# Retention scores by 8 products of 64x128 instead of 16 on quarters of the array, with the keys in their order

## The chip, the cores and the metric

The kernel runs on one core of a Trainium2 chip. The metric is device time in microseconds (us) for one execution of the whole program. One execution was also profiled: its trace tells for each engine when each instruction began and ended and what it waited for.

## What is computed

Retention attention for 8 batches, 8 heads, 576 tokens and 64 numbers a head, then a layer of 8 experts on the result, in float32:

```python
scores = scale * np.matmul(q, k.transpose(0, 1, 3, 2))
gamma = 1.0 - 2.0 ** (-5.0 - np.arange(H, dtype=np.float32))
rel = pos[:, None] - pos[None, :]
Dmat = np.where(rel >= 0, gamma[:, None, None] ** rel[None, :, :], 0.0)
ret = scores * Dmat[None, :, :, :]
x = np.matmul(ret, v)                       # then tokens x 512
# experts: rows with x @ w_skip > 0 go to the expert e with the largest x @ w_gate,
# and get x + gate * (relu(x @ w1[e]) @ w2[e]); the others stay x
```

## The kernel before

The 8 x 576 = 4608 tokens are 36 tiles of 128 tokens (NT). Nine tiles (NPD) hold one pair of sequences, so the middle tile of a pair (place 4) holds the end of one sequence and the start of the next. Each tile g is one step of a loop that is unrolled in the program; the order of the TensorE instructions is the order in which the program is written. After the 36 steps, at about 150 us, come the experts, which take the rest of the time and which the change leaves alone.

A step g issues to TensorE, in this order: `state(g)` (L668, keys by values, summed into the state of the sequence; it does nothing at the last tile of a pair), `values(g)` (L688, masked scores by values), `carried(g)` (L709, the state of earlier tiles by queries; it does nothing at the first tile of a pair), `scores(g + 2)` (L618, keys by queries), `stage_c(g - 1)` (L739, four transposes of the finished tile to rows), `flush` (L234, L237, L322, L332: routing matmuls that VectorE has prepared), `logits_b` (L762, four transposes, in every fourth step) and `logits_a` (L747, in every fourth step). VectorE multiplies the scores by the causal mask on their way from the accumulators psc to SBUF (`causal`) and the results by the decay (`decayed`), and does the routing in the time between. GpSimd scales the values (`scale`, L653). ScalarE copies the state, the transposed rows (L741, and sends them to HBM) and the logits lt (L756).

The scores of a step are 8 heads with 64 numbers each. Two heads share the 128 partitions (r = 0, 1, the upper and the lower 64 rows of the array), and for each of four such pairs (a) the 128 keys are taken in two halves of 64 (c), so that 16 products of 64 keys by 128 or 64 queries use the four 64x64 quarters of the array; a half of the keys that lies behind the first 64 queries is left out (k0). For odd a the keys' halves are swapped: `rows` swaps the tokens of k and v on the host, `_tables` swaps the decay of the values, and the mask has a second plane for it. A float32 product is two MATMUL instructions, each with a load of weights, in the trace.

Loads: `load` sends one DMA of 512 KB for q and k by head (n = 0, six buffers) and one for v and k by token (n = 1, four buffers), on SP's queue in the order of the program: v of tile g + 4 after `values(g)`, q of tile g + 6 after `carried(g)`. The keys by token are read by `state` alone.

Of the kernel before, what the change touches and what calls it, by code (L numbers as in the profile page):

```python
# [11 lines left out]
F32 = mybir.dt.float32  # L12
# [5 lines left out]
ALU = mybir.AluOpType  # L18
# [3 lines left out]
B, H, S, D = 8, 8, 576, 64  # L22
NTOK, DM, NE, DF = B * S, H * D, 8, 1024
P = 128
NT = NTOK // P
NQ = S // D
NPR = H // 2
NPD = 2 * S // P
# [41 lines left out]
def kernel(  # L70
# [9 lines left out]
    nc = tc.nc  # L80
# [15 lines left out]
    def keep_up(n):  # L96
        for _ in range(n):
            nc.tensor.matmul(ps_m, warm[:, :P], warm, start=True, stop=True)
# [26 lines left out]
        out=utri, in_=utri, compare_op=ALU.is_gt, fill=0.0, base=0, pattern=[[1, P]], channel_multiplier=-1  # L125
# [56 lines left out]
    def vec(name, *args, **kw):  # L182
        ins = getattr(nc.vector, name)(*args, **kw)  # L183
        if pinned[0]:
            tc.keep_in_program_order(ins)
        return ins
# [6 lines left out]
    def flush(most=None):  # L193

        n = len(adds) if most is None else most
        for do in pe + adds[:n]:
            do()
        pe.clear()
        del adds[:n]
        flushed[0] += 1  # L200
# [342 lines left out]
    with ExitStack() as actx:  # L543
        ac = actx.enter_context(tc.tile_pool(name="ac", bufs=1))
# [9 lines left out]

        q_t, v_t = {}, {}

        def load(into, n, g):
            into[g] = ap.tile([P, 2, DM], F32, tag="qv"[n], name=f"{'qv'[n]}_{g}", bufs=(QBUFS, VBUFS)[n])
            nc.sync.dma_start(into[g].rearrange("p s i -> p (s i)"), qkv[g, n])

        load(q_t, 0, 0)
        nc.scalar.dma_start(tt_sb, ttab)
        load(v_t, 1, 0)
# [9 lines left out]
        masks = []  # L573

        def make_mask(n):
            m = ac.tile([P, 2, P], F32, tag=f"mask{n}", name=f"mask{n}")
            tc.keep_in_program_order(nc.gpsimd.memset(m, 1.0))
            for e in range(2):
                for c in range(2):
                    part = m[c * D : (c + 1) * D, e, :]  # L580
                    if n and c == e:
                        tc.keep_in_program_order(nc.gpsimd.memset(m[c * D : (c + 1) * D, e, D:], 0.0))
                        part = m[c * D : (c + 1) * D, e, :D]
                    ins = nc.gpsimd.affine_select(
                        out=part,
                        in_=part,
                        compare_op=ALU.is_ge,
                        fill=0.0,
                        base=-D if c != e else 0,
                        pattern=[[1, part.shape[-1]]],  # L590
                        channel_multiplier=-1,
                    )
                    tc.keep_in_program_order(ins)
            masks.append(m)

        make_mask(0)
# [2 lines left out]
        halves = [slice(0, D), slice(D, P)]  # L599
        sc_t, st_t, xt_t = {}, {}, {}  # L600
        psc = [pp.tile([P, NPR, P], F32, tag=f"sc{r}", name=f"psc{r}") for r in range(2)]
        for r in range(2):
            nc.vector.memset(psc[r], 0.0)

        def head(a, r):
            return 2 * a + (r ^ (a & 1))

        def place(g):
            return g % NPD

        def scores(g):

            q = q_t[g].rearrange("p s (a i) -> p s a i", a=NPR)
            for a in range(NPR):
                for c in range(2):
                    k0 = D * (c ^ (a & 1))
                    for r in range(2):
                        nc.tensor.matmul(  # L618
                            psc[r][halves[c], a, k0:],
                            q[halves[r], 1, a, k0 : k0 + D],  # L620
                            q[halves[r], 0, a, k0:],
                            start=a == 0,
                            stop=a == NPR - 1,
                            skip_group_check=True,
                        )

        def causal(g):

            sc_t[g] = ap.tile([P, 2, NPR, P], F32, tag="sc", name=f"sc_{g}", bufs=AHEAD_SC + 1)
            m = masks[place(g) == NPD // 2].unsqueeze(1).broadcast_to([P, NPR // 2, 2, P])  # L630
            for r in range(2):
                vec(
                    "tensor_tensor",
                    sc_t[g][:, r].rearrange("p (b e) i -> p b e i", e=2),
                    psc[r].rearrange("p (b e) i -> p b e i", e=2),
                    m,
                    ALU.mult,
                )
# [21 lines left out]
        def state(g):  # L660

            t = place(g)
            if t == NPD - 1:
                return
            v, k = (v_t[g][:, s].rearrange("p (h i) -> p h i", h=H) for s in range(2))
            for a in range(NPR):
                for r in range(2):
                    nc.tensor.matmul(  # L668
                        ps_s[halves[r], a, :],
                        k[:, head(a, r), :],  # L670
                        v[:, head(a, r), :],
                        start=t in (0, NPD // 2) and a == 0,
                        stop=a == NPR - 1,
                        skip_group_check=True,
                    )
            st_t[g + 1] = ap.tile([P, NPR, D], F32, tag="st", name=f"st_{g + 1}")
            nc.scalar.copy(st_t[g + 1], ps_s)
# [149 lines left out]
        def lower_whole(f):  # L827
            hi, lo = wq[0, f]
            vec("tensor_tensor", lo, chunks[f], hi.bitcast(F32), ALU.subtract)
# [14 lines left out]
        def closed(b, pn):  # L844

            logits_c(b, pn)
            if (b + 1) * NB in starts:
                k = starts.index((b + 1) * NB) - 1
                post = (lambda: close_first(ps_m, starts[KCUT + 1] * P)) if k == KCUT else None
                work.append(route(ps_m, k, post))  # L850
# [18 lines left out]
        for g in range(NT):  # L869
            last = g >= NT - 2  # L870
            if g < len(NKEEP):
                keep_up(NKEEP[g])
            state(g)
            pxt = values(g)
            if g == NT - 3:
                lower_whole(3)
            if g + VBUFS < NT:
                load(v_t, 1, g + VBUFS)
            carried(g, pxt)
            if g + QBUFS < NT:  # L880
                load(q_t, 0, g + QBUFS)
            old = len(adds) if g < (KCUT + 4) * NB else None
            if last:
                decayed(g, pxt)
            if pn is not None:
                closed(g // NB - 1, pn)
                pn = None
            if g < NT - 1:
                spare(SPARE if g < (KCUT + 4) * NB else LATE)
            if not last:  # L890
                first = decayed(g, pxt)
                scale(g + 2, first)
                lower(1, first)
            if g == NT - 3:
                lower_whole(4)
            score(g + (AHEAD_SC if g > 2 else 1))
            if g < 4:
                decays(g + 1)
            if g:
                stage_c(g - 1)  # L900
            if g != NT - 2:
                flush(old)
            if lt is not None:
                pn = logits_b(g // NB - 1, lt)
                lt = None
            if g and g % NB == 0:
                lt = logits_a(g // NB - 1)
            weights()
        g = NT
# [509 lines left out]
def _tables():  # L1419
    gam = 1.0 - 2.0 ** (-5.0 - np.arange(H, dtype=np.float64))  # L1420
    a = np.arange(NPR)
    gtab = np.zeros((P, 2, NPR, D))
    qtab = np.zeros((P, NQ + 1, NPR))
    off = D * (np.arange(NQ + 1) % NQ - np.arange(NQ + 1) % 2)
    for j in range(2):
        mine = slice(j * D, (j + 1) * D)
        g = gam[2 * a + j]
        for c in range(2):
            gtab[mine, c] = g[None, :, None] ** (c * D + np.arange(D))[None, None, :] / np.sqrt(D)
        qtab[mine] = g[None, None, :] ** off[None, :, None]  # L1430
    pos = np.arange(NPD * P).reshape(NPD, P) % S
    vtab = gam[None, None, :] ** -pos.T[:, :, None]
    odd = np.arange(H) // 2 % 2 == 1
    vtab[:, :, odd] = np.roll(vtab, D, axis=0)[:, :, odd]
    f = np.float32
    ttab = np.concatenate([vtab.reshape(P, -1), qtab.reshape(P, -1)], axis=1)
    return gtab.reshape(P, DM).astype(f), ttab.astype(f)
# [41 lines left out]
```

## Time and profile before

| | us |
|---|---|
| median of 3 runs | 395.24 |
| lowest and highest | 391.83, 397.61 |
| the profiled execution | 394.96 |
| its span, first to last instruction | 393.3 |

The span is shorter than the execution by 1.7 us that lie around it. In the rows further below, times are us from the span's start unless marked ns. PE is TensorE's matmuls, PEld its loads of weights, DVE VectorE, ACT ScalarE, POOL GpSimd, SP SyncE; a name with q is the engine's sequencer or DMA queue. L618 is line 618 of the kernel before. "x16" is a count of instructions. Matmuls overlap, so a group's time from its own start to the start of the next group is a better measure of what it costs than its busy time.

### The profile page before, as it was taken

How to read it: one execution, taken by the hardware profiler on the slowest of the kernel's cores; microseconds unless marked ns; L12 is line 12 of the kernel's file. 1: busy time of each engine (PE TensorE's matmuls, PEld its weight loads, DVE VectorE, ACT ScalarE, POOL GpSimd, SP SyncE). 2: the span in 40 equal slices, each digit the busy share in tenths (PEclk: the TensorE clock that was granted, in tenths of full speed). 3: DMA queues.
4: the chain of work that ended last, by engine and by line, in shares of the span. 5: the costliest groups of instructions: out<-in, count | busy, mean ns of one | idle time of the engine just before them, and what ended most of it. 6: DMA issues, size and time to landing. Idle time of an engine off the chain costs nothing.

```text
span 393.3 us, 11952 instructions
## 1 busy us (share of the span) xinstructions
PE 376.0 (96%) x4792; PEld 342.1 (87%) x4792; DVE 280.4 (71%) x690; ACT 149.6 (38%) x258; POOL 162.0 (41%) x183
## 2 busy tenths in 40 slices
PE   8889999999899999999999999999999999999992
PEld 4768788787787877888999999999999999999992
DVE  3765695596379998967753887597787887977625
ACT  1222322232234435128432545445445455464210
POOL 5532232223144463160123347328448348660712
PEclk9999999999899999999999999999999999999998
DMA  8999999999999936175899997687877878973101
GB/s 301 405 413 351 354 343 310 391 353 319 412 323 350 358 112 215 67 243 153 259 317 258 300 245 201 241 231 243 250 236 255 219 247 271 254 236 122 48 9 58
DMA packets 41001, 101.00 MB, mean 257 GB/s; under 512 B 5165, under 2 KB 14129, under 8 KB 40944
## 3 DMA queue, kind: packets, MB, share of 16 engines
q1 hardware_dynamic: 31440, 80.62, 62.5%
q0 software_dynamic: 4032, 10.03, 7.7%
q10 hardware_dynamic: 5472, 9.56, 6.5%
q8 instruction: 39, 0.64, 0.7%
q14 instruction: 18, 0.15, 0.1%
HBM read 81.49 MB, written 19.21 MB: 256 GB/s over the span
## 4 chain that ended last, share of the span: by engine, by line
PE 88%; DVE 5%; DMA 3%; issue 2%; ACT 1%; SPq 0%; POOL 0%; DVEq 0%
PE py L507 28%; PE ph L507 25%; PE pxt L688 8%; PE psc L618 6%; PE ps_s L668 5%; PE px L739 5%; PE pxt L709 4%; PE pl L747 2%; DMA v<-qkv 2%; DMA w<-w 1%; PE ps_m L322 1%; DVE sc L183 1%; PE ph L532 1%; PE pn L762 1%; DVE xt L183 1%
## 5 line engine op out<-in xcount | busy, mean ns | idle before, releaser
L1139 POOL DMA_INDIRECT out<-yq,siq x60 | 72.8, 1213 | 51.0 <-DVE yq L1118 26.7
L170 ACT CAST whi_w<-w 128x1024 fp32r<-128x1024 f32 x59 | 61.8, 1050 | 36.9 <-PE py L507 35.2
L653 POOL TENSOR_TENSOR v<-v,tt_sb 128x512 f32<-128x512 f32 x36 | 37.6, 1043 | 91.4 <-DVE xt L183 67.9
L171 DVE TENSOR_TENSOR wlo_w<-w,whi_w 128x1024 fp32r<-128x1024 f32 x59 | 71.2, 1210 | 2.1 <-ACT whi_w L170 2.1
L507 PE MATMUL py<-hlo,whi_w 128*128 128x344 f32 (+8 forms) x232 | 69.9, 301 | 0.4 <-DVE hlo L520 0.4
L507 PE MATMUL py<-hhi,whi_w 128*128 128x344 f32 (+8 forms) x232 | 69.8, 301 | 0.0
L507 PE MATMUL py<-hhi,wlo_w 128*128 128x344 f32 (+8 forms) x232 | 69.6, 300 | 0.0
L507 PE MATMUL ph<-xhi,whi_w 128*128 128x344 f32 (+6 forms) x224 | 67.8, 303 | 0.0
L507 PE MATMUL ph<-xhi,wlo_w 128*128 128x344 f32 (+6 forms) x224 | 67.7, 302 | 0.0
L507 PE MATMUL ph<-xlo,whi_w 128*128 128x344 f32 (+6 forms) x224 | 67.6, 302 | 0.0
L520 DVE SCALAR_TENSOR_TENSOR hlo<-ph,hhi 128x344 fp32r<-128x344 f32 (+8 forms) x60 | 28.5, 474 | 43.6 <-ACT hhi L519 43.5
L183 DVE TENSOR_TENSOR sc<-psc,mask 128x512 f32<-128x512 f32 x72 | 46.3, 684 | 10.5 <-PE psc L618 6.4
L741 ACT COPY xn<-px 128x512 f32<-128x512 f32 x36 | 21.1, 586 | 82.0 <-PE px L739 73.7
L183 DVE TENSOR_TENSOR xt<-pxt,gt_sb 128x256 f32<-128x256 f32 x72 | 27.0, 417 | 31.8 <-PE pxt L709 29.1
L519 ACT ACTIVATE hhi<-ph 128x344 fp32r<-128x344 f32 (+8 forms) x60 | 25.6, 426 | 57.9 <-PE ph L507 57.9
L420 POOL DMA_INDIRECT xg<-out,gidx x21 | 26.3, 1253 | 47.6 <-issue 27.4
L507 PEld LDWEIGHTS py<-hlo,whi_w 128*128 128x128 f32 x232 | 43.7, 188 | 0.7 <-DVE hlo L520 0.7
L507 PEld LDWEIGHTS py<-hhi,wlo_w 128*128 128x128 f32 x232 | 43.8, 189 | 0.0
L507 PEld LDWEIGHTS py<-hhi,whi_w 128*128 128x128 f32 x232 | 43.7, 188 | 0.0
L507 PEld LDWEIGHTS ph<-xhi,whi_w 128*128 128x128 f32 x224 | 42.2, 188 | 0.1
L507 PEld LDWEIGHTS ph<-xlo,whi_w 128*128 128x128 f32 x224 | 42.1, 188 | 0.1
L507 PEld LDWEIGHTS ph<-xhi,wlo_w 128*128 128x128 f32 x224 | 42.2, 188 | 0.0
(203 smaller groups left out, 601.7 us busy)
## 6 DMA issues: line engine op xcount, KB each, us to landing
w<-w SPq DMA_DIRECT2D x64, 512.0 KB, 4.3
q<-qkv SPq DMA_DIRECT2D x36, 512.0 KB, 7.5
v<-qkv SPq DMA_DIRECT2D x36, 512.0 KB, 6.7
out<-xn ACTq DMA_DIRECT2D x36, 256.0 KB, 5.5
xr<-xg SPq DMA_DIRECT2D x7, 512.0 KB, 5.3
xq<-xr SPq DMA_DIRECT2D x12, 144.0 KB, 4.6
xq<-xr SPq DMA_DIRECT2D x8, 176.0 KB, 5.4
xq<-xr SPq DMA_DIRECT2D x8, 160.0 KB, 6.9
```

The source lines that it names most:

```text
L170: nc.scalar.copy(hi, t)
L171: ins = nc.vector.tensor_tensor(lo, t, hi.bitcast(F32), ALU.subtract)
L183: ins = getattr(nc.vector, name)(*args, **kw)
L420: return nc.gpsimd.indirect_dma_start(out=dst, out_offset=None, in_=out[:nrow], in_offset=bass.IndirectOffsetOnAxis(ap=idx, axis=0), bound ...
L507: nc.tensor.matmul(ps, x, y, start=first and n == 0, stop=ends, skip_group_check=skip)
L519: nc.scalar.activation(hi, ph, AF.Relu)
L520: keep(nc.vector.scalar_tensor_tensor(lo, ph, 0.0, hi.bitcast(F32), ALU.max, ALU.subtract))
L618: nc.tensor.matmul(psc[r][halves[c], a, k0:], q[halves[r], 1, a, k0 : k0 + D], q[halves[r], 0, a, k0:], start=a == 0, stop=a == NPR - 1, s ...
L653: ins = nc.gpsimd.tensor_tensor(v, v, vt_sb[:, place(g), :].unsqueeze(2).broadcast_to([P, H, D]), ALU.mult)
L688: nc.tensor.matmul(pxt[a % 2][halves[j], a // 2, :], v[:, head(a, r), :], sc[:, r, a, :], start=a < 2, stop=t == 0 and a >= NPR - 2, skip_ ...
L741: nc.scalar.copy(xn, px)
L1139: ins = nc.gpsimd.indirect_dma_start(out=dst, out_offset=bass.IndirectOffsetOnAxis(ap=idx, axis=0), in_=rows, in_offset=None, bounds_check ...
```

## The change

The scores become 8 products of 128 keys by 128 queries: for each a and r one product on a 64x128 half of the array, with no part left out. The mask becomes one plane of 128x128, built with one selection. The swap of the keys' halves for odd a goes, on the host (rows of k and v, the decay table) and in the mask; the memsets that cleared the accumulators psc go too. `logits_b` is issued ahead of `flush` instead of behind it. The last tile of each pair (place 8, four of the 36 tiles) loads only v, half of the former transfer.

```diff
         def load(into, n, g):
             into[g] = ap.tile([P, 2, DM], F32, tag="qv"[n], name=f"{'qv'[n]}_{g}", bufs=(QBUFS, VBUFS)[n])
-            nc.sync.dma_start(into[g].rearrange("p s i -> p (s i)"), qkv[g, n])
+            m = 1 if n and place(g) == NPD - 1 else 2
+            nc.sync.dma_start(into[g][:, :m, :].rearrange("p s i -> p (s i)"), qkv[g, n, :, : m * DM])
...
-            m = ac.tile([P, 2, P], F32, tag=f"mask{n}", name=f"mask{n}")
+            m = ac.tile([P, P], F32, tag=f"mask{n}", name=f"mask{n}")
             tc.keep_in_program_order(nc.gpsimd.memset(m, 1.0))
...
+            ins = nc.gpsimd.affine_select(
+                out=m, in_=m, compare_op=ALU.is_ge, fill=0.0, base=0, pattern=[[1, P]], channel_multiplier=-1
+            )
+            tc.keep_in_program_order(ins)
+            if n:
+                tc.keep_in_program_order(nc.gpsimd.memset(m[:D, D:], 0.0))
...
-        for r in range(2):
-            nc.vector.memset(psc[r], 0.0)
...
             for a in range(NPR):
-                for c in range(2):
-                    k0 = D * (c ^ (a & 1))
-                    for r in range(2):
-                        nc.tensor.matmul(
-                            psc[r][halves[c], a, k0:],
-                            q[halves[r], 1, a, k0 : k0 + D],
-                            q[halves[r], 0, a, k0:],
...
+                for r in range(2):
+                    nc.tensor.matmul(
+                        psc[r][:, a, :],
+                        q[halves[r], 1, a, :],
+                        q[halves[r], 0, a, :],
...
-            m = masks[place(g) == NPD // 2].unsqueeze(1).broadcast_to([P, NPR // 2, 2, P])
+            m = masks[place(g) == NPD // 2].unsqueeze(1).broadcast_to([P, NPR, P])
...
-            if g != NT - 2:
-                flush(old)
             if lt is not None:
                 pn = logits_b(g // NB - 1, lt)
                 lt = None
+            if g != NT - 2:
+                flush(old)
...
-    odd = np.arange(H) // 2 % 2 == 1
-    vtab[:, :, odd] = np.roll(vtab, D, axis=0)[:, :, odd]
...
-        odd = np.arange(H) // 2 % 2 == 1
-        return np.where(odd[:, None], np.roll(x, D, axis=1), x).reshape(NT, P, DM)
+        return x.reshape(NT, P, DM)
```

## Rows read from the trace of the kernel before

**Rows 1.** The page: its span, and busy us (share of span) with instructions.

```profile
span 393.3 us, 11952 instructions
PE 376.0 (96%) x4792; PEld 342.1 (87%) x4792; DVE 280.4 (71%) x690; ACT 149.6 (38%) x258; POOL 162.0 (41%) x183
```

**Rows 2.** The page: the chain of work that ended last, by engine.

```profile
PE 88%; DVE 5%; DMA 3%; issue 2%; ACT 1%; SPq 0%; POOL 0%; DVEq 0%
```

**Rows 3.** Stretches: length, each engine's busy time (instructions), granted clock, DMA share, GB/s.

```profile
20.00:146.00 126.00, 120.26 (x2753) 99.64 (x2754) 90.33 (x253) 38.69 (x76) 40.71 (x42) 0.99 0.92 338
...
100.00:120.00 20.00, 18.22 (x396) 15.54 (x397) 11.38 (x34) 6.28 (x12) 6.24 (x7) 0.91 0.98 369
```

**Rows 4.** Waits of TensorE, 20 to 146 us: total, times, longest.

```profile
PE psc L618 <- issue: 4.6, 5, 1.8
PE psc L618 <- DVE sc L183: 1.0, 2, 0.8
```

**Rows 5.** Timeline of TensorE in a clean step: start, length, group.

```profile
53.05 0.67 PE L709 MATMUL pxt<-q,st 64*64 64x128 f32 x16
53.53 0.85 PE L618 MATMUL psc<-q 64*64 64x128 f32 x32
54.31 0.66 PE L739 MATMUL px<-ident,xt 128*128 128x128 f32 x4
54.90 0.39 PE L668 MATMUL ps_s<-v 128*64 128x64 f32 x6
```

**Rows 6.** Timeline of TensorE in a step without L709.

```profile
45.17 1.05 PE L688 MATMUL pxt<-sc,v 128*64 128x128 f32 x16
46.14 0.90 PE L618 MATMUL psc<-q 64*64 64x128 f32 x32
46.98 0.33 PE L739 MATMUL px<-ident,xt 128*128 128x128 f32 x1
```

**Rows 7.** Timeline of TensorE in the last steps, some without scores.

```profile
143.74 0.66 PE L739 MATMUL px<-ident,xt 128*128 128x128 f32 x4
144.23 0.60 PE L762 MATMUL pn<-ident,lt 128*128 128x128 f32 x4
...
146.25 0.67 PE L709 MATMUL pxt<-q,st 64*64 64x128 f32 x16
146.85 0.66 PE L739 MATMUL px<-ident,xt 128*128 128x128 f32 x4
```

**Rows 8.** Timeline around the longest idle stretch of TensorE (in brackets).

```profile
100.42 0.85 PE L618 MATMUL psc<-q 64*64 64x128 f32 x31
...
103.05 0.27 PE L618 MATMUL psc<-q 64*64 64x128 f32 x1 [1.78 <-issue]
...
103.25 1.11 PE L739 MATMUL px<-ident,xt 128*128 128x128 f32 x4
```

**Rows 9.** The page: the instruction queue's packets, MB, share of 16 engines.

```profile
q8 instruction: 39, 0.64, 0.7%
```

**Rows 10.** Instructions of L618 from 20 to 146 us: duration, first and last.

```profile
L618 PE MATMUL psc<-q x1024: 212/267/320, 20.4 to 143.6; 64*64 64x64 f32 x98, 64*64 64x128 f32 x73
```

**Rows 11.** Timeline of the start, GpSimd and VectorE.

```profile
3.59 1.29 POOL L584 TENSOR_SCALAR_AFFINE_SELECT mask<-mask 64x128 f32<-64x128 f32 x4
...
6.41 1.04 POOL L653 TENSOR_TENSOR v<-v,tt_sb 128x512 f32<-128x512 f32 x1 [1.52 <-DMA v<-qkv]
6.46 1.29 DVE L183 TENSOR_TENSOR sc<-psc,mask 128x512 f32<-128x512 f32 x2 [4.11 <-issue]
```

**Rows 12.** Timeline: ScalarE's copy of the logits, and their transposes.

```profile
90.52 0.59 ACT L756 COPY lt<-pl 128x512 f32<-128x512 f32 x1 [0.44 <-PE pl L747]
...
93.63 0.60 PE L762 MATMUL pn<-ident,lt 128*128 128x128 f32 x4
```

More of the change, by code (lines that the diff above doesn't have):

```diff
@@ L555, with place @@
         q_t, v_t = {}, {}
+        def place(g):
+            return g % NPD
         def load(into, n, g):
             into[g] = ap.tile([P, 2, DM], F32, tag="qv"[n], name=f"{'qv'[n]}_{g}", bufs=(QBUFS, VBUFS)[n])
-            nc.sync.dma_start(into[g].rearrange("p s i -> p (s i)"), qkv[g, n])
+            m = 1 if n and place(g) == NPD - 1 else 2
+            nc.sync.dma_start(into[g][:, :m, :].rearrange("p s i -> p (s i)"), qkv[g, n, :, : m * DM])
         load(q_t, 0, 0)
@@ L575, in make_mask @@
         def make_mask(n):
-            m = ac.tile([P, 2, P], F32, tag=f"mask{n}", name=f"mask{n}")
+            m = ac.tile([P, P], F32, tag=f"mask{n}", name=f"mask{n}")
             tc.keep_in_program_order(nc.gpsimd.memset(m, 1.0))
-            for e in range(2):
-                for c in range(2):
[L580 to L593, printed above, removed]
+            ins = nc.gpsimd.affine_select(
[4 more added lines that the diff above has]
+                tc.keep_in_program_order(nc.gpsimd.memset(m[:D, D:], 0.0))
             masks.append(m)
@@ L601 @@
         psc = [pp.tile([P, NPR, P], F32, tag=f"sc{r}", name=f"psc{r}") for r in range(2)]
-        for r in range(2):
-            nc.vector.memset(psc[r], 0.0)
         def head(a, r):
             return 2 * a + (r ^ (a & 1))
-        def place(g):
-            return g % NPD
         def scores(g):
@@ L614, in scores @@
             for a in range(NPR):
-                for c in range(2):
-                    k0 = D * (c ^ (a & 1))
-                    for r in range(2):
-                        nc.tensor.matmul(
-                            psc[r][halves[c], a, k0:],
-                            q[halves[r], 1, a, k0 : k0 + D],
-                            q[halves[r], 0, a, k0:],
[L622 to L625, printed above, removed]
+                for r in range(2):
[3 more added lines that the diff above has]
+                        q[halves[r], 0, a, :],
+                        start=a == 0,
+                        stop=a == NPR - 1,
+                        skip_group_check=True,
+                    )
         def causal(g):
             sc_t[g] = ap.tile([P, 2, NPR, P], F32, tag="sc", name=f"sc_{g}", bufs=AHEAD_SC + 1)
-            m = masks[place(g) == NPD // 2].unsqueeze(1).broadcast_to([P, NPR // 2, 2, P])
+            m = masks[place(g) == NPD // 2].unsqueeze(1).broadcast_to([P, NPR, P])
             for r in range(2):
@@ L633, in causal @@
                     "tensor_tensor",
-                    sc_t[g][:, r].rearrange("p (b e) i -> p b e i", e=2),
-                    psc[r].rearrange("p (b e) i -> p b e i", e=2),
+                    sc_t[g][:, r],
+                    psc[r],
                     m,
```

## The prediction

> **What bounds the kernel now.** First the page's busy times and its chain: TensorE is busy for 376.0 of 393.3 us, and 88% of the chain that ended last is TensorE [rows 1, 2]. So the question is what the change does to TensorE's own queue, and, since it edits only the retention stage, in the tile steps of the first 150 us. The table by stretches shows the steps between 20 and 146 us: TensorE busy 120.26 of 126 us, granted clock 0.99, DMA share 0.92 [rows 3]. Both are near full, so it has to be settled which is waited for. TensorE's list of waits for the same stretch answers: 4.6 us before products of L618 that nothing in the profile released ("issue"), 1.0 us for VectorE's masking, and no line for a load [rows 4]. Loads are late at times, but never late enough for TensorE. The steps are paced by TensorE's instruction stream, and I price the change there.
>
> Now one clean step, read from the starts of TensorE's groups: L709 at 53.05, L618 at 53.53, L739 at 54.31, L668 at 54.90 [rows 5]. The score products hold the queue for 54.31 - 53.53 = 0.78 us, the carried-state products (L709) ahead of them for 0.48. A step without L709 shows L688 from 45.17 to 46.14 = 0.97 us, then L618 from 46.14 to 46.98 = 0.84 [rows 6].
>
> **The shape of the score products.** Before, a step's scores are 32 matmuls (16 calls, two each in float32) on four 64x64 quarters of the array, 64 or 128 queries each. A quarter gets 4 x 2 passes, half of 128 columns and half of 64: 8 x 96 = 768 columns. After, 16 matmuls on two 64x128 halves, all of 128 queries: 8 x 128 = 1024 columns per half. The trace of before has no 64x128 product. The nearest row is L688: also 16 matmuls of 128 columns on two tiles, 0.97 us [rows 6]. From below, no row allows less than the present 0.78, since the columns per tile grow by a third; from above, halves that don't run together would take twice L688, 1.94. I take 0.97: the four quarters of L618 run together today, among them both row halves (32 matmuls in 0.78), which two halves also need. That is 0.97 - 0.78 = +0.19 us a step.
>
> **The change of shape in front.** Today L709 and L618 both use 64x64 tiles. After, L709's 64x64 is followed by 64x128. Where the next group has another shape, a group's tail shows in the rows: L709 ahead of L739 takes 146.85 - 146.25 = 0.60 instead of 0.48, and L739 ahead of L762 (same shape) takes 0.49 against 0.59 ahead of L668, where only the columns of the tile differ [rows 5, 7]. And the group behind a change starts slower: L618 behind L688 takes 0.84, behind L709 0.78 [rows 5, 6]. So a new change of shape costs 0.12 + 0.06 = 0.18 us; from below it costs 0, if tiles of equal rows can follow each other freely, which no row shows. I take 0.18, because L739 to L668 is also a change of columns alone. The Trainium skill has the rule (TensorEngine Tiling (Array Packing), Key Properties): a change of tiling mode, unlike a change of tile within one mode, drains the array. By that rule the 64x64 to 64x128 step drains, which is the value that the rows led to; taken without it the sum would be 5.4 us lower.
>
> **How often.** 36 sets of score products are issued. The first two lie in front of TensorE's wait for the first two loads and cost nothing; if they were on the path, +0.4. Of the 34 others, 30 stand behind L709 (+0.37 each = 11.1), three behind L688, at the tiles that start a sequence pair (+0.19 = 0.6), one behind another set (+0.2): **+11.9 us**. Without the drain 34 x 0.19 = +6.5.
>
> **The gaps.** The 4.6 us of "issue" are five idle stretches, all inside or just ahead of L618, the longest 1.78 [rows 4, 8]. They cost more than their idle time, since the work around them no longer overlaps: the set at 100.42 ends at 103.25, 2.83 - 0.78 = 2.05 for 1.78 idle [rows 8]. I take that surplus, 0.27, for each of the five, an estimate: 4.6 + 1.3 = 5.9. Right behind the longest gap the clock drops: in 100 to 120 us the granted clock is 0.91 [rows 3], so 0.09 x 20 = 1.8 us of full clock are lost, of which I count 1.7. What are the gaps? Nothing releases them, and they fall in the densest part of the instruction stream: 64 instructions (32 loads of weights, 32 matmuls) in 0.78 us. The page lists an instruction queue with 39 packets, 0.64 MB [rows 9], and TensorE has 2 x 4792 = 9584 matmuls and weight loads [rows 1]: if that queue is TensorE's own, 246 in a packet of 16 KB. I read the gaps as late instruction packets, held up in the DMA queues that are 92% busy. Between 20 and 146 us TensorE issues 2753 + 2754 instructions [rows 3], 246 in 5.6 us; after, 1024 fewer (half of the 1024 matmuls of L618 and as many loads [rows 10]) in about 132 us, 246 in 7.2. Each packet has some 1.6 us more to arrive, nearly the longest gap. I take the gaps as gone: **-5.9 - 1.7 = -7.6 us**. From below nothing is regained: 0.
>
> **Costed at nothing.** (a) Four of the 36 v loads bring half: 1 MB less on SP's queue, the order of issue unchanged. It is hidden because TensorE waits for no load [rows 4]; if loads set the pace it would be worth 1.05 MB at 338 GB/s, 3.1 us. (b) The memsets of psc on VectorE and most of the mask on GpSimd (1.29 us) go. GpSimd's first scaling waits 1.52 us for a load behind the mask, and VectorE is idle for 4.11 us ahead of its first masking [rows 11]; without that cover the gain would be about the 1.29 us once. (c) Masking has the same 128x512 elements and the mask is only broadcast differently: 0.65 us as before (1.29 for two [rows 11]); were it slower, VectorE is idle for 126 - 90.33 = 35.7 us between 20 and 146 us, or 1 us a step [rows 3]. (d) logits_b moves ahead of the routing matmuls of flush, on TensorE alone; it issues no DMA. It needs ScalarE's copy lt, which starts at 90.52 and takes 0.59, long before the transposes at 93.63 [rows 12]. Behind it now wait the routing matmuls, 0.5 us later in 8 of 36 steps; their accumulator is read a step or more later. Should lt be late, the whole queue would stand behind it. (e) A longer step gives VectorE, GpSimd and the loads time; it takes none.
>
> **Sum**, against the profiled execution's own 394.96 us (span 393.3; the median of the runs is 395.24, 0.3 more): 394.96 + 11.9 - 7.6 = 399.3 us, +1.1%. Without the drain and with the gaps gone 394.96 + 6.5 - 7.6 = 393.9; with the drain and no gap regained 406.9.
>
> **Rivals.** *The gaps stay* (slower). If the gaps are not owed to the density of L618's instructions, only the costs remain: 394.96 + 11.9 = 406.9, +3%. It decides from about 4 us of gaps kept. For it: the profile names no releaser, and DMA stays above 90% busy. Against: all five lie at L618. The Trainium skill (Runtime: NRT & Kernel Launch, Instruction fetch mechanics) says that instruction fetch is mostly hidden, so that by it the gaps would have another cause and could stay; the rows above place them at the densest stretch, which speaks rather for fetch. *The halves run one after the other* (much slower): 0.97 more a set, 34 x 0.97 = 33, 432 us; against it stands the overlap of the quarters now. *The loads set the pace* (faster): then TensorE's extra time is hidden, 3.1 us of loading and the gaps go: 394.96 - 3.1 - 7.6 = 384.3. Against: no TensorE wait for a load [rows 4]. *No change of shape is felt, or the changes cancel*: 394, inside the forecast's side.
>
> **Chances.** Forecast, costs and regained gaps between 392 and 402.9: 0.55. Gaps stay, wholly or mostly: 0.27. Halves in turn: 0.06. Loads or something else that gives over 2%: 0.12. The likeliest case's own range is 393 to 404; for 8 in 10 I go to 388 below and 408 above, which leaves out the halves in turn and most of the faster case. About 2% (7.9 us) is what a measurement of this kernel can tell from no change: faster 0.11, within 0.56, slower 0.33 (gaps stay, halves in turn).
>
> **What would show it.** L618 with 16 matmuls of 64x128, start to next start near 1.03 us (0.97 + 0.06); L709 ahead of it 0.60; "issue" before L618 under 1 us in all, and no half clock after 20 us; the instruction queue with about 4 or 5 packets fewer (1152 of TensorE's instructions). Wrong would be: L618 at 0.8 or 1.9; gaps of the same sum, at L618 or elsewhere; a new TensorE wait for v or q.

## The result and the profile after

The changed kernel takes 399.39 us (median of 20 runs, 398.55 to 400.24), the kernel before beside it 396.2 (20 runs, 391.83 to 399.89): ratio 1.0095, interval 1.0074 to 1.0116. It is about 1% slower, within the 2% that counted as no change. The profiled execution takes 398.64 us, 3.7 more than that of before. The experiments further below ran on other chips, where the kernel before itself scattered between 394.1 and 412 us; so they are read by their traces first, and by a ratio only where one is given with its interval.

The page after: span, busy time, the instruction queue, the chain that ended last.

```profile
span 396.9 us, 10793 instructions
PE 385.0 (97%) x4216; PEld 347.9 (88%) x4216; DVE 280.0 (71%) x688; ACT 150.0 (38%) x258; POOL 162.6 (41%) x176
...
q8 instruction: 34, 0.56, 0.6%
...
PE 91%; DMA 3%; DVE 2%; issue 1%; ACT 1%; POOL 1%; SPq 0%; DVEq 0%
```

TensorE lost 576 matmuls and 576 loads of weights, the instruction queue 5 packets [rows 1, 9]. VectorE's share of the chain fell from 5% to 2% [rows 2]. Now the tile steps, by stretches as in [rows 3], and TensorE's waits from 20 to 146 us as in [rows 4]:

```profile
20.00:146.00 126.00, 125.04 (x2178) 101.63 (x2178) 88.31 (x245) 37.12 (x74) 38.60 (x40) 1.00 0.91 328
100.00:120.00 20.00, 20.00 (x364) 16.61 (x360) 12.18 (x33) 5.91 (x12) 6.27 (x7) 1.00 1.02 400
```

```profile
PE psc L605 <- DVE sc L183: 0.8, 1, 0.8
```

The 4.6 us of idle time that nothing released are gone, all of them, and with them the drop of the clock: 1.00 in 100 to 120 us, where it was 0.91. TensorE is busy for 125.04 of 126 us instead of 120.26. And still the program is longer, because each step is. A clean step after (L696 is the former L709, L605 the former L618, L726 the former L739, L655 the former L668):

```profile
55.66 0.67 PE L696 MATMUL pxt<-q,st 64*64 64x128 f32 x16
56.26 1.16 PE L605 MATMUL psc<-q 64*128 64x128 f32 x16
57.35 0.66 PE L726 MATMUL px<-ident,xt 128*128 128x128 f32 x4
57.94 0.45 PE L655 MATMUL ps_s<-v 128*64 128x64 f32 x8
```

From start to next start, the carried products take 0.60 us (0.48 before) and the score set 57.35 - 56.26 = 1.09 (0.78 before) [rows 5]. Behind the values' products, where there are no carried ones, the set takes 1.10 (0.84 before, [rows 6]):

```profile
48.07 1.16 PE L605 MATMUL psc<-q 64*128 64x128 f32 x16
49.17 0.65 PE L726 MATMUL px<-ident,xt 128*128 128x128 f32 x4
```

What a set's single instructions last (shortest, median, longest, ns), first before, then after:

```profile
L618 PEld LDWEIGHTS psc<-q x1024: 129/133/136, 20.3 to 143.5; 64*64 64x64 f32 x171
```

```profile
L605 PEld LDWEIGHTS psc<-q x512: 182/188/188, 21.7 to 147.9; 64*128 64x128 f32 x171
L605 PE MATMUL psc<-q x512: 272/272/373, 21.7 to 148.0; 64*128 64x128 f32 x171
```

A load of 128 columns lasts some 53 ns longer than one of 64. In the middle of a set this is hidden behind matmuls; at its start, behind a change of shape, it is not, and the longest matmuls, the first of a set, last 373 ns where they lasted 320 [rows 10].

Where the difference ends: the first product of the experts starts at 154.01 us before and at 158.33 after, 4.3 us later. The profiled executions differ by 3.7, so 0.6 are made up in the experts; where in them was not looked for.

```profile
154.01 0.50 PE L507 MATMUL ph_early<-x,whi_w 128*128 128x256 f32 x2 [0.39 <-DVE x L183]
```

```profile
158.33 0.48 PE L507 MATMUL ph_early<-x,whi_w 128*128 128x256 f32 x2
```

### The profile page after: what moved, and what is told of

It reads as the page before. It is cut to its first block, busy times and chain, and to the rows that moved or that the text cites. A ratio compares the mean times of both kernels' runs of the same rounds, so it can differ in the third digit from the quotient of the medians.

```text
span 396.9 us, 10793 instructions
## 1 busy us (share of the span) xinstructions
PE 385.0 (97%) x4216; PEld 347.9 (88%) x4216; DVE 280.0 (71%) x688; ACT 150.0 (38%) x258; POOL 162.6 (41%) x176
## 4 chain that ended last, share of the span: by engine, by line
PE 91%; DMA 3%; DVE 2%; issue 1%; ACT 1%; POOL 1%; SPq 0%; DVEq 0%
PE py L507 28%; PE ph L507 25%; PE psc L605 9%; PE pxt L675 7%; PE px L726 5%; PE ps_s L655 5%; PE pxt L696 4%; PE pl L734 2%; DMA v<-qkv 2%; DMA xg<-out,gi 1%; PE ph_early L507 1%; PE pn L749 1%; PE ph L532 1%; PE ps_m L322 1%; DVE sc L183 0%
## 5 line engine op out<-in xcount | busy, mean ns | idle before, releaser
L1126 POOL DMA_INDIRECT out<-yq,siq x60 | 74.7, 1245 | 56.2 <-DVE yq L1105 28.9
L605 PE MATMUL psc<-q 64*128 64x128 f32 x576 | 42.3, 285 | 1.0 <-DVE sc L183 0.8
```

The lines of the kernel that those rows point to most:

```text
L605: nc.tensor.matmul(psc[r][:, a, :], q[halves[r], 1, a, :], q[halves[r], 0, a, :], start=a == 0, stop=a == NPR - 1, skip_group_check=True,)
L1126: ins = nc.gpsimd.indirect_dma_start(out=dst, out_offset=bass.IndirectOffsetOnAxis(ap=idx, axis=0), in_=rows, in_offset=None, bounds_check ...
```

## The experiments

Three things had to be told apart: whether the products alone carry the change; whether the shape or the columns make them dearer; and what the idle gaps were. Theory on the gaps: TensorE uses up its instructions faster than packets of them arrive. Rivals: they belong to the products on quarters, or the loads alone make them.

**The rest of the change alone.** The kernel before, with the half loads and `logits_b` ahead of `flush`; scores, masks and layout as before.

```diff
+            m = 1 if n and g % NPD == NPD - 1 else 2
+            nc.sync.dma_start(into[g][:, :m, :].rearrange("p s i -> p (s i)"), qkv[g, n, :, : m * DM])
...
             if lt is not None:
                 pn = logits_b(g // NB - 1, lt)
                 lt = None
+            if g != NT - 2:
+                flush(old)
```

> The kernel before with two parts of the change alone: the half loads of the last tile of a pair and the logits' transposes ahead of the flush; the score products stay on quarters. Theory (the score products carry the whole change): no difference that can be measured, ratio 1.000, TensorE's idle gaps of the kernel before still there (2 to 8 us). Rival (the other parts give something that hides part of the products' cost): 3 us faster (0.992), the price of 1 MB of loads.

Its waits from 20 to 146 us:

```profile
PE psc L619 <- issue: 3.0, 3, 2.1
PE psc L619 <- DVE sc L183: 1.0, 2, 0.8
PE pxt L710 <- issue: 0.4, 1, 0.4
```

The gaps are still there, 3.4 us. The profiled execution took 397.9 us, the kernel before in the same session 396.4 at its lowest. Too few runs could be compared for an interval, so a gain of 3 us is not excluded by the times. The trace shows none: TensorE waits for no load here either. The first product of the experts does start 2.5 us earlier than in the kernel before, but 1.2 us less of gaps and a clock that does not drop (it cost 1.7 us in the kernel before) cover that:

```profile
151.47 0.51 PE L507 MATMUL ph_early<-x,whi_w 128*128 128x256 f32 x2 [0.40 <-DVE x L183]
```

**The same columns on quarters.** The changed kernel with each score product cut in two by its keys: 64x64 again, so no change of shape behind the carried products, but 1024 columns per tile.

```diff
             for a in range(NPR):
-                for r in range(2):
+                for c in range(2):
+                    for r in range(2):
...
-                        psc[r][:, a, :],
-                        q[halves[r], 1, a, :],
-                        q[halves[r], 0, a, :],
+                            psc[r][halves[c], a, :],
+                            q[halves[r], 1, a, halves[c]],
+                            q[halves[r], 0, a, :],
```

> The changed kernel with each score product cut in two by its keys: 16 products of 64 keys by 128 queries on quarters, so again 64x64 like the carried-state products ahead of them, 32 matmuls, but the 1024 columns per tile of the change. Theory (of the 0.43 us a step that the products cost, 0.19 are columns and 0.24 the change of shape and its exposed first load): the carried products 0.48 instead of 0.60, the score set 0.97 instead of 1.09, 30 x 0.24 = 7 us less, 392 us, if the idle gaps stay away; with as many instructions as before some may come back, up to 8 us, then 392 to 400. Rival (the change of shape costs nothing, the columns and the larger weights cost all): score set 1.09, carried 0.60, 399 us.

> 16 products of 64 keys by 128 queries on quarters, all else as in the changed kernel, again, because the first time the runs were disturbed. Theory (change of shape 0.22 us a step, read from the first profile; its instruction rate is nearly that of the kernel before, so gaps of 2 to 4 us): 30 x 0.22 = 6.6 less than the changed kernel, 2 to 4 given back: 3 to 5 us under the changed kernel, ratio to the kernel before about 0.995 to 1.005. Rival (shape costs nothing over the whole program, the next step absorbs it): as the changed kernel, 1.01.

A clean step, from the second profile:

```profile
50.96 0.67 PE L697 MATMUL pxt<-q,st 64*64 64x128 f32 x16
51.45 1.05 PE L606 MATMUL psc<-q 64*64 64x128 f32 x32
52.44 0.65 PE L727 MATMUL px<-ident,xt 128*128 128x128 f32 x4
```

The carried products take 0.49, the set 0.99, together 1.48. With the change it is 1.69, before 1.26. So of the 0.43 us that a step got longer, 0.22 are the third more columns (1.48 - 1.26) and 0.21 the change of shape with its exposed first load (1.69 - 1.48). The load's own part shows behind the values' products, where the shape changes either way (128x64 to 64x64 here, to 64x128 with the change):

```profile
47.41 1.10 PE L606 MATMUL psc<-q 64*64 64x128 f32 x32
48.45 0.66 PE L727 MATMUL px<-ident,xt 128*128 128x128 f32 x4
```

With first loads of 64 columns the set takes 1.04 us there, with 128 columns 1.10: 0.06 for the larger load. The gaps came back in part, in the second profile 1.7 us:

```profile
PE px L727 <- issue: 1.5, 1, 1.5
PE psc L606 <- DVE sc L183: 1.0, 2, 0.8
PE pxt L676 <- issue: 0.2, 1, 0.2
```

In the first session the ratio to the kernel before was 1.0032 (0.9928 to 1.0136, from two runs of this kernel), in the second 1.0068 (1.0019 to 1.0117), just above the upper end of what was expected. The changed kernel itself, beside it in the second session:

> The changed kernel once more, beside the next two, on their chip. Theory: TensorE waits on nothing that the profile does not release before the scores (under 0.5 us of issue between 20 and 146 us), score set 1.09, carried products 0.60, and a ratio to the kernel before of 1.005 to 1.015. Rival (the absence of gaps in the first profile was luck): 2 us of gaps or more.

It came to 1.012 (1.0053 to 1.0188), without a gap in 20 to 146 us, as in its first profile. By medians the quarters with all columns take 2.9 us less (399.36 against 402.24), where 6.6 - 1.7 = 4.9 would be left; the two intervals overlap, so the times alone do not show a difference. What the shape costs is read from the steps.

**More instructions, same shape.** The changed kernel with each product of scores by values cut in two by queries: as many instructions per step as before.

```diff
-                    nc.tensor.matmul(
-                        pxt[a % 2][halves[j], a // 2, :],
-                        v[:, head(a, r), :],
-                        sc[:, r, a, :],
-                        start=a < 2,
+                    for h in range(2):
+                        nc.tensor.matmul(
+                            pxt[a % 2][halves[j], a // 2, halves[h]],
+                            v[:, head(a, r), :],
+                            sc[:, r, a, halves[h]],
+                            start=a < 2 and h == 0,
```

> The changed kernel with each product of scores by values cut in two by queries: 32 matmuls of 64 queries and 32 loads of weights instead of 16 and 16, same columns, same shape, so the instruction count per step is that of the kernel before while the score products stay 64x128. Theory (the gaps are late instruction packets, owed to the density): idle gaps that nothing releases come back, each behind an instruction packet, 1 to 5 us in all, at the dense stretch wherever that now is; 400 to 404 us and a wider spread from run to run. Rival (the gaps belonged to the quarter products themselves or to chance): none, spread as narrow as with the change (under 2 us), 399 to 400 us, if the group of values stays at 0.98 us.

```profile
20.00:146.00 126.00, 125.04 (x2498) 106.09 (x2497) 82.11 (x225) 34.17 (x69) 34.90 (x36) 1.00 0.89 320
```

This missed: no gap came back, and the time rose to between 411.9 and 425.3 us (four runs; the kernel before beside it 396.4 to 412.0). The cut was not free, as had been assumed: the group of values takes 1.24 us instead of 0.98:

```profile
57.73 1.31 PE L676 MATMUL pxt<-sc,v 128*64 128x64 f32 x32
58.97 0.67 PE L697 MATMUL pxt<-q,st 64*64 64x128 f32 x16
```

So the step got longer with its instructions, and the pace fell: 4995 instructions in 126 us, 246 in 6.2 us, against 5.4 before outside its gaps. The count per step alone does not make the gaps. That left two readings, the pace or the quarters, and the next pair tells them apart.

**Products on quarters at a slower pace.** The kernel of the first experiment, where each tile's transposes to rows are issued two or three times with the same result.

```diff
-            for c in range(NCC):
+            for c in 2 * list(range(NCC)):
                 nc.tensor.transpose(px[:, c * P : (c + 1) * P], xt_t[b][:, c, o * P : (o + 1) * P], ident)
```

> The kernel before (with the half loads and the logits' order), score products on quarters as before, each tile's four transposes to rows issued twice with the same result: 8 more instructions and 0.44 us more TensorE time a step, so TensorE uses 246 instructions in about 5.8 us instead of 5.5 to 5.65. Theory (the gaps are late packets, and what counts is how fast TensorE uses up a packet): gaps of 0.5 to 2.5 us in 20 to 146 us. Rival (gaps belong to the quarter products, whatever the pace): 3 to 5 us, as before.

> As the one before, each transpose issued three times: 0.9 us more a step, 246 instructions in about 6.1 us, the pace at which the kernel with the values' products cut in two had no gap. Theory: under 0.5 us of gaps. Rival (quarter products): 3 to 5 us.

Twice, the stretch and its waits:

```profile
20.00:146.00 126.00, 123.41 (x2742) 105.99 (x2737) 85.58 (x239) 35.13 (x70) 37.14 (x39) 1.00 0.91 327
```

```profile
PE psc L619 <- DVE sc L183: 1.0, 2, 0.8
PE pxt L689 <- issue: 0.9, 1, 0.9
PE ps_s L669 <- issue: 0.7, 1, 0.7
```

Three times:

```profile
20.00:146.00 126.00, 124.96 (x2628) 109.11 (x2626) 76.48 (x209) 32.82 (x66) 33.39 (x34) 1.00 0.88 313
```

```profile
PE psc L619 <- DVE sc L183: 1.0, 2, 0.9
```

With the same products on quarters the gaps shrink to 1.6 us at the slower pace, none of them at the scores, and are gone at the slowest. So they do not belong to the products on quarters; they follow the pace. With each transpose issued twice the pace fell less than expected, to 246 instructions in 5.59 us instead of 5.8. All kernels in a row, as the time in which TensorE used 246 instructions in 20 to 146 us while it did not stand in a gap (126 us less the gaps, by matmuls and weight loads):

| kernel | instructions | gaps, us | us per 246 | DMA share |
|---|---|---|---|---|
| before | 5507 | 4.6 | 5.42 | 0.92 |
| rest alone | 5593 | 3.4 | 5.39 | 0.92 |
| five buffers for q (below) | 5473 | 5.4 | 5.42 | 0.90 |
| weights later (below) | 5506 | 5.5 | 5.38 | 0.90 |
| all columns on quarters, second profile | 5504 | 1.7 | 5.56 | 0.90 |
| the same, first profile | 5464 | 2.1 | 5.58 | 0.89 |
| transposes twice | 5479 | 1.6 | 5.59 | 0.91 |
| transposes three times | 5254 | 0 | 5.90 | 0.88 |
| values cut in two | 4995 | 0 | 6.21 | 0.89 |
| after | 4356 | 0 | 7.12 | 0.91 |
| after, once more | 4356 | 0 | 7.12 | 0.89 |
| lighter loads (below) | 5663 | 2.0 | 5.39 | 0.80 |

At an almost equal DMA share, the last row aside, the gaps depend on the pace: several us at 5.4, about 2 at 5.6, none from 5.9 on. Each row is one profile.

**Where the gaps lie.** That they are packets of instructions can be read from the traces by counting. In the kernel before, the columns as in [rows 3], between the middles of its five gaps, and the instruction queue from 20 to 146 us:

```profile
39.20:72.70 33.50, 32.51 (x759) 27.26 (x759) 23.35 (x65) 9.68 (x20) 8.93 (x9) 1.00 0.97 342
72.70:84.60 11.90, 11.35 (x253) 9.25 (x253) 8.53 (x29) 3.34 (x7) 3.13 (x3) 1.00 0.99 378
84.60:96.40 11.80, 11.36 (x253) 9.16 (x253) 9.20 (x29) 3.47 (x7) 3.13 (x3) 1.00 0.91 316
96.40:102.20 5.80, 4.54 (x127) 4.10 (x127) 3.85 (x10) 0.96 (x2) 2.05 (x2) 1.00 1.01 398
```

```profile
q8 instruction: 22, 0.36, 1.2%
```

From gap to gap TensorE uses 759 + 759 = 6 x 253 matmuls and loads, then 2 x 253 twice, then 254; and the queue brings 22 packets for 5507 of them, one per 250. The same holds in every profile: all 29 idle stretches that nothing released, in the eight profiles that have any, lie on one series of counts from the program's start with steps of 253 or 254 (within three instructions), whichever product stands there, and each ends 1.2 to 1.6 us after a packet of the instruction queue has ended. So each gap is TensorE at the end of one packet with the next not yet there, and a packet holds about 253 of its instructions, not 246.

**Lighter loads.** The kernel before without the loads of keys by token. The state products multiply the values by themselves, so the result is another; only the first 150 us are read.

```diff
-            nc.sync.dma_start(into[g].rearrange("p s i -> p (s i)"), qkv[g, n])
+            m = 1 if n else 2
+            nc.sync.dma_start(into[g][:, :m, :].rearrange("p s i -> p (s i)"), qkv[g, n, :, : m * DM])
...
-            v, k = (v_t[g][:, s].rearrange("p (h i) -> p h i", h=H) for s in range(2))
+            v = k = v_t[g][:, 0].rearrange("p (h i) -> p h i", h=H)
```

> The kernel before without the loads of keys by token: the state products multiply the values by themselves, so 256 KB of the 1 MB of loads a step go, and the result and the later routing are not the reference's; only the first 150 us are read. Same TensorE instructions as before. Theory (the packets are late because the loads keep the DMA queues full): DMA share falls from 0.92 to about 0.7, and the gaps that nothing releases fall from 4.6 us to under 1. Rival (gaps owed to the instruction count or the products alone): gaps of 3 to 6 us stay.

```profile
20.00:146.00 126.00, 122.73 (x2833) 101.85 (x2830) 94.04 (x269) 40.09 (x79) 42.72 (x45) 1.00 0.80 273
```

```profile
99.49 0.27 PE L619 MATMUL psc<-q 64*64 64x128 f32 x1 [2.04 <-issue]
```

At the pace of before (5663 instructions, 246 in 5.39 us) one gap of 2.0 us is left of five; as far as one profile tells, the loads have a part in the others, but the expected "under 1" failed. The one that is left stands in front of the last matmul of the same score set as the 1.78 us in [rows 8].

**Two attempts to keep the cheap products and lose the gaps.** Both start from the kernel of the first experiment: `QBUFS = 5` instead of 6, and each early load of expert weights held until VectorE's decay of its step (`load_w(0, len(chunks), regs, first)`).

> The kernel before with the half loads and the logits' order of the change, and five buffers for q instead of six, so that each load of q is asked for one step later. Theory (late packets stand behind transfers that are in flight, and fewer are in flight): gaps fall from 3 to 4.6 us to 1 or 2, 1 to 3 us faster than the kernel before (0.993 to 0.998). Rival (the DMA rings are as full with five): gaps of 3 to 5 us, ratio 1.000; a load that now comes late would show as a new wait of TensorE before the scores.

> The kernel before with the half loads and the logits' order of the change, and each of the five early loads of expert weights (512 KB) held until VectorE's decay of its own step; in the kernel before four of them start between 91 and 102 us, just ahead of the longest gap. Theory (that gap comes from these loads on top of the others): the gap at about 100 us falls from 2 us to under 0.5 and the clock does not drop there, 2 to 4 us faster than the kernel before (0.990 to 0.995). Rival (the packet of that stretch is late for another reason): the gap of about 2 us stays at the same place in the program, ratio 1.000.

Ratios 0.9995 (0.9943 to 1.0048) and 1.0031 (0.9987 to 1.0075): neither does anything that can be measured. The waits of the second:

```profile
PE psc L619 <- issue: 2.9, 3, 1.5
PE ps_m L237 <- issue: 1.4, 1, 1.4
PE pxt L710 <- issue: 1.2, 2, 1.0
```

Both theories fell: with one load fewer asked for ahead the gaps are 5.4 us, with the weights later 5.5, and in both the last matmul of that same set is 1.5 us late:

```profile
102.47 0.27 PE L619 MATMUL psc<-q 64*64 64x128 f32 x1 [1.51 <-issue]
```

No version beat the kernel before.

## Why the prediction was right

*The bound*, TensorE's own queue in the steps: right. After, TensorE is busy for 125.04 of 126 us and no load is waited for.

*The shape of the products*: right that the two halves run together. The set was taken at 0.97 + 0.06 = 1.03 us and measured 1.09. The term that was too small is the slow start behind a change of shape. It was read from a set that loads 64 columns of weights; the new set loads 128, and its first load stands open (1.10 against 1.04 us behind the values' products).

*The change of shape in front*: right, 0.60 for the carried products, to the hundredth. The Trainium skill's rule that a change of tiling mode drains the array (TensorEngine Tiling (Array Packing), Key Properties) holds here from 64x64 to 64x128, which no row of before showed; the quarters with all columns, without that change, took 0.21 us a step less.

*How often*: the step came out 0.43 us longer, not 0.37. With 30 steps of 0.43, three sets of 0.26 and the pair of sets at 0.2 the cost is 13.9 us instead of 11.9.

*The gaps*: right in size (all 4.6 us went) and in kind: they are late instruction packets, as the counts show, and the pace at which TensorE uses up its instructions makes them, as the pair with repeated transposes shows at the same products. Three things in the reading did not hold. That all five lay at L618 was taken as a sign of its density; they lie where a packet ends, in other profiles at L237, L669, L689 or L710. Packets are not late only because the loads fill the queues, since one gap of 2 us outlived a DMA share of 0.80. And the 1.7 us for the clock were luck: the profiled execution of before had a drop behind its longest gap, but four other profiles with a gap of 1.5 to 2.1 us at the same place had none. The Trainium skill has instruction fetch mostly hidden (Runtime: NRT & Kernel Launch, Instruction fetch mechanics). These traces agree at 246 instructions in 5.9 us and slower, where no packet is waited for; at 5.4 us, in the kernel before, five of 22 packets were.

*The sum*: 399.3 was forecast and the profiled execution took 398.6. That it came so near is luck: two errors cancel. The steps cost 2 us more than forecast. Between the first steps and the experts 4.3 of the 13.9 us are left, so 9.6 were regained where 7.6 were counted. Some of the other 2.0 is VectorE: before, TensorE's routing matmuls waited for it in places, and a longer step takes these waits in. Before:

```profile
123.35 1.16 PE L322 MATMUL ps_m<-mc,r 128*128 128x40 bf16 x15
124.44 1.07 PE L747 MATMUL pl<-xt,wg_sb 128*32 128x512 f32 x8
```

After:

```profile
126.67 0.53 PE L322 MATMUL ps_m<-mc,r 128*128 128x40 bf16 x15
127.13 1.07 PE L734 MATMUL pl<-xt,wg_sb 128*32 128x512 f32 x8
```

The same 15 matmuls took 1.09 us from start to next start and now take 0.46. The prediction had said of a longer step that it gives VectorE time, and priced that at nothing. TensorE's 0.39 us of waiting for VectorE ahead of the first product of the experts (the line at 154.01 above) went too.

*Costed at nothing*: the traces agree for the half loads and the logits' order, since no gain shows with the rest alone, and for the masking, 684 ns before and 685 after on average. The new mask and the missing memsets were not tried alone; the first products of scores by values start at 7.84 us instead of 8.02, which is all that shows of them. The rivals fell: the gaps did not stay, the halves did not run in turn, the loads did not set the pace.

One thing more that the gaps explain, argued and not shown: the 20 runs of before lie 8.1 us apart, those of after 1.7. Gaps that differ from execution to execution would do that, and the profiles above show 3.4 to 5.5 us of them at one pace. Against it speaks the changed kernel on the second chip: its profiled execution took 406.02 us without a gap, two others 401.4, so something else can move the time as much.

What stays open: why TensorE stands for 1.5 to 2.1 us at that one place in kernels of the old instruction count, whatever the loads do. The place itself is explained: 4241 instructions lie ahead of it, so a packet ends there in all of them (with all columns on quarters the gap comes one instruction later, ahead of L727). The transfer of the next packet lasts 0.9 to 1.0 us there, but begins only 0.2 to 1.0 us before TensorE runs out (at 100.84 us for 101.27 in the kernel before). Why it begins so late, no run shows.

## What to carry to other kernels

Price a change of a matmul's shape from start to next start of neighbouring groups, and count three things: the columns per tile, the tail of the group in front if its tile shape differs, and the first load of weights, which stands open and grows with its columns. Idle time of TensorE that nothing released, in a stretch of many small matmuls, can be instructions arriving late: count TensorE's instructions from one idle stretch to the next, where multiples of one number point to packets, and compare the pace (instructions per us) before looking for a missing semaphore. Fewer instructions win that time back only as far as the larger products don't cost more: here 7 to 8 us regained stood against 14.

## What the runs showed that had not been expected

With 64-column weights and 64 moving columns on two 128x64 tiles (the values cut in two) 32 matmuls took 1.24 us where 16 with 128 columns took 0.98: the same columns, 27% more time. In the kernel before, the clock dropped to 1.2 GHz, the lower of its two levels, right behind the gap of 1.78 us: granted clock 0.50 from 103.3 to 106.7 us, 1.7 us of full clock lost. The gaps of 2.07 us in the rest alone, 2.04 with lighter loads and 1.51 with the weights later were followed by no drop (granted clock 1.00 from 20 to 146 us). And DMA share is a poor sign of what the loads cost TensorE: it stood at 1.02 in 100 to 120 us after the change, without one wait.
